# An attention and feed-forward kernel whose first product is done with seven block products in four of six chunks

## The chip, the cores and the metric

The kernel runs on one core of a Trainium2 chip. A core has TensorE (PE, matrix products; PEld is its loading of weights), VectorE (DVE), ScalarE (ACT), GpSimd (POOL) and SyncE (SP), which issues most transfers. SBUF is the working memory of 128 partitions, PSUM the memory of eight banks into which TensorE writes. The metric is the device time of one execution in microseconds; less is better.

## The reference

A local attention with block summaries is followed by a feed-forward layer without a choice of experts. Cut to what matters:

```python
# q, k, v: (4, 8, 768, 64); w_in: (512, 2048); w_out: (2048, 512)
k_sum = k.reshape(B, H, 24, 32, D).max(axis=3)
v_sum = v.reshape(B, H, 24, 32, D).mean(axis=3)
scores_l = q @ k.T / 8, kept where |i - j| < 16
scores_s = q @ k_sum.T / 8 + log(32)
a = softmax(concat(scores_l, scores_s))
x = (a @ concat(v, v_sum)) as (3072 tokens, 512)
h = x @ w_in
g = h * erf(softplus(h))
out = g @ w_out
```

All data are float32, and the output is too.

## The kernel before

**Tiles.** The 3072 tokens are cut into six chunks of T = 512, and the 2048 hidden columns into four groups of 512. A period k stands for one chunk and one group (ch = k // 4, g = k % 4), so there are 24 periods. A unit of weights is 128x2x512, half a megabyte in float32; each is held as two fp32r parts, high and low, 1 MB for both together.

**Products.** The first product `mm1(k, f)` makes h transposed: 128 hidden columns (f = 0 to 3) by 512 tokens, summed over four parts of x (cc = 0 to 3). Each part costs three matmuls, high by high, high by low and low by high, so a period has 4 x 4 x 3 = 48 matmuls of 128x512 at L635. The second product `mm2(k)` adds to four banks o0 to o3 with 48 more at L700; in the first two periods it is done in plain f32 with fewer matmuls (L696). The four results of mm1 go alternately into the banks h0 and h1; `hout` (L640) copies them to the tile hc, 128x1024 for two of them (n = 0, 1).

**Between the products.** softplus(h) is made of Tanh (L650), Ln (L659) and then Erf (L664) on ScalarE; Exp for the softmax (L541) runs on it too. They need different function tables, which L899 loads. `gsplit` multiplies by h on VectorE (L676), casts to the high part gh (L275) and subtracts for the low part gl (L683). hc, gh and gl have one buffer for each half n, so gh of a period can be written only when the second product of the period before has read it.

**Attention.** A quad is one chunk and one pair of heads, 24 in all. Each period from k = 4 to 19 turns, applies and splits quad k + 4 (`transp`, L571; `av`, L596; `xsplit`, L602 to L614) and scores quad k + 5 (`scores`, L500; `softmax`, L517 to L561). Scores and turned probabilities share a double bank, pa; av writes into h0 or h1. xsplit leaves x as xh and xl for each head pair.

**Order.** Each operation is registered in a `Plan` with its engines and planned cost, and with names that it reads and writes. `Plan.order` (L100) places them one at a time, by the engine that is free first, and by a due time (L79) plus a shift from the table TUNE (L44). TensorE's operations may leave their order of registration by up to 60 places among the first 330, and not at all afterwards. Every engine's queue is then executed in that order. In periods 4 to 23 TensorE's registered order is mm1 with attention between, and then mm2 of the period before (L843 to L870).

**Weights.** SBUF has 14 slots, w0 to w13. w_in stays in w0 to w7. Of w_out, parts m = 0 to 3 stay in slots from period 4 or 5 on; m = 4 to 7 go to DRAM once (`put`, L355) and come back into the slots 10 and 8 (`get`, L363) when the second product has read what was there.

**End.** After the last period mm2 runs alone, and `evac_last` (L718) copies and stores the output in halves.

Of the kernel before, what the change touches and what calls it, by code (L numbers as in the profile page):

```python
# [40 lines left out]
NN = 2  # L41
TABLE = 1.29
# [10 lines left out]
class Plan:  # L53
# [6 lines left out]
    def add(self, eng, fn, r=(), w=(), after=(), table=None, hold=0.0, beside=None):  # L60


        n, deps = len(self.ops), set(after)
        for x in r:
# [12 lines left out]
        return n  # L77
# [107 lines left out]
def block_attention_mlp(ctx: ExitStack, tc: tile.TileContext, q_t, k_nat, k_win, v_tok, v_nat, v_win, w_in, w_out, out):  # L185
# [87 lines left out]

    def copy(e, o, i):
        e.copy(o, i) if e is nc.scalar else e.tensor_copy(o, i)  # L275
# [79 lines left out]
    def put(m, n):  # L355
        u = ("o", m // 2, m % 2)

        def go():
# [4 lines left out]
    def get(m):  # L363
        u, n = ("o", m // 2, m % 2), HOME[m]

        def go():
            t = slot(n, [128, 2, 2, 512], F32R, "w")
            whl[u] = t[:, 0], t[:, 1]
            nc.sync.dma_start(out=f32(t), in_=dr[m])
        dma(1049, go, [f"d{m}"], frees(n), hold=0.0)  # L370


    rows = sb([128, 2 * S], F32, "rows")
# [228 lines left out]
    def xsplit(qd, eng):  # L602
        ch, p = divmod(qd, NP)
        n, s = qd % NX, st[qd]

        def high(e):
            xt[ch, p] = [sb([128, T], F32R, m, f"{m}{n}") for m in ("xh", "xl")]
            copy(e, xt[ch, p][0], s["xo"])

        def low(e):  # L610
            st.pop(qd)
            e.tensor_tensor(xt[ch, p][1], s["xo"], f32(xt[ch, p][0]), op=ALU.subtract)
        on(eng, high, [s["bank"]], [f"xh{n}"])
        on({"DVE": 0.6}, low, [s["bank"], f"xh{n}"], [f"xl{n}"])  # L614


    hs, wt, hc, gs, os_ = {}, {}, {}, {}, {}
# [22 lines left out]
    def hout(k, f, eng):  # L640
        bank, s = hbank(k, f), f // 2

        def hcopy(e):
            if f % 2 == 0:
                hc[k, s] = sb([128, 2, T], F32, "hc", f"hc{s}")
            copy(e, hc[k, s][:, f % 2], hs[k, f][:, 0:T])

        def tanh():
            wt[k, s] = sb([128, 2, T], F32, "wt", f"wt{s}")
            nc.scalar.activation(wt[k, s], hc[k, s], AF.Tanh, scale=0.5)  # L650
        on(eng, hcopy, [bank], [f"hc{s}"])
        if f % 2:
            act(0.96, tanh, [f"hc{s}"], [f"wt{s}"], table=("sig", "exp"))

    def logs(k):

        for n in range(2):
            s = f"wt{n}"
            act(1.06, lambda n=n: nc.scalar.activation(wt[k, n], wt[k, n], AF.Ln, scale=-0.49999994, bias=half_b), [s], [s], table=("log",))  # L659

    def erfs(k, after):
        for n in range(2):
            s = f"wt{n}"
            act(0.96, lambda n=n: nc.scalar.activation(wt[k, n], wt[k, n], AF.Erf, scale=-1.0), [s], [s], table=("sig",), after=after)  # L664
# [23 lines left out]
    def mm2(k, fs=range(G), ts=range(NT)):  # L688
        ch, g = divmod(k, NG)

        def go(i, t):
            if g == 0 and i == 0:
                os_[ch, t] = tiles[f"o{t}"] = ps("ops", f"o{t}")
            x, first, last = gs[k, i // 2], g == 0 and i == 0, g == NG - 1 and i == G - 1
            if k < NN:
                nc.tensor.matmul(os_[ch, t], lhsT=x[0][:, i % 2, t * 128:(t + 1) * 128], rhs=w32["o", g, i // 2][:, i % 2], start=first, stop=last)  # L696
                return
            w = [t[:, i % 2] for t in whl["o", g, i // 2]]
            for n, (m, y) in enumerate(((0, 0), (0, 1), (1, 0))):
                nc.tensor.matmul(os_[ch, t], lhsT=x[y][:, i % 2, t * 128:(t + 1) * 128], rhs=w[m], start=first and n == 0, stop=last and n == 2)  # L700
        for i in fs:
            for t in ts:
                m = 2 * g + i // 2
                if k < NN:
                    pe(0.868, lambda i=i, t=t: go(i, t), [f"a{m}", f"gh{i // 2}"], [f"o{t}"])
                else:
                    pe(0.681, lambda i=i, t=t: go(i, t), [f"w{HOME[m] if ch else FIRST[m]}", f"gh{i // 2}", f"gl{i // 2}"], [f"o{t}"])

# [102 lines left out]
    early = 5  # L811
    early_att = {(1, 1): [(lambda n: follow(n, "o2"), 4)], (1, 3): [(attend, 4), (follow, 5)],
                 (2, 1): [(output, 4), (attend, 5), (follow, 6)], (2, 3): [(output, 5), (attend, 6), (follow, 7)],
                 (3, 1): [(output, 6), (attend, 7), (follow, 8)], (3, 3): [(output, 7), (attend, 8), (follow, 9)]}

    for k in range(NPER):
        qa, qs = k + NP, k + NP + 1
        ch, g = divmod(k, NG)
        mult = sub = {"DVE": 1.136}
        cast = {"DVE": 0.605}  # L820
# [8 lines left out]
        if k == 4:  # L829
            parts(0, 9)  # L830
        if k == 5:
            for m in (1, 2, 3):
                parts(m, HOME[m])
        if k < NG:
            for f in range(G):
                if k and f % 2 == 0:
                    gsplit(k - 1, f // 2, mult, cast, sub)
                if k:
                    mm1(k, f)
                hout(k, f, heng)  # L840
                for what, n in early_att.get((k, f), []):
                    what(n)
        else:  # L843
# [17 lines left out]
            if qa < NQ:  # L861
                xsplit(qa, xeng)
# [6 lines left out]
        if k:  # L869
            mm2(k - 1)  # L870
# [70 lines left out]
```

## Time and profile before

| | us |
|---|---|
| median of 3 runs | 638.03 |
| lowest and highest | 636.91, 638.83 |
| profiled execution, first to last instruction (span) | 635.3 |
| TensorE busy in it | 629.0 |
| VectorE busy | 392.0 |
| ScalarE busy | 431.7 |
| POOL busy | 19.6 |

The span lies 2.7 us under the median of the runs: it counts from the first to the last instruction. Of the 24 periods the ones from k = 8 to 18 take about 25 us each, and the last ones, without attention, 21.8. In a row of groups stand line, engine, operation, tile, shape and count; then busy time and the mean of one instruction, and the idle time ahead of them. In the chain, start and length stand ahead of engine, tile and line. In a row of windows stand the limits and the length, the busy time of the five engines in order, the granted clock, the DMA engines' share and GB/s.

### The profile page before, as it was taken

What the parts mean: (1) busy time and instruction counts of PE and PEld (TensorE: products, weight loads), DVE (VectorE), ACT (ScalarE), POOL (GpSimd) and SP (SyncE); (2) the same over time, 40 slices, a digit from 0 to 9 for tenths busy, and PEclk for the clock granted to TensorE, in tenths of its full rate; (3) what the DMA queues carried; (4) which work ended last, traced back from release to release, by engine and by line L of the source; (5) the groups of instructions that cost most, each with busy time, mean ns of one, the idle gap of its engine ahead of it and who ended that gap; (6) DMA issues with size and microseconds to landing.
All of it is one profiled execution on the core that took longest, in us unless ns stands there. A gap on an engine that the chain in (4) does not pass through costs nothing.

```text
span 635.3 us, 10484 instructions
## 1 busy us (share of the span) xinstructions
PE 629.0 (99%) x4264; PEld 502.0 (79%) x4264; DVE 392.0 (62%) x502; ACT 431.7 (68%) x742; POOL 19.6 (3%) x56
## 2 busy tenths in 40 slices
PE   8999999999999999999999999999999999999997
PEld 6776557888888887888888888888888888888886
DVE  4999999756766647676655645735555454334442
ACT  5669977978949648976484684674954952863470
POOL 2001010100000000000000000000000000000000
PEclk9999999999999999999999999999999999999999
DMA  9998947724641334653152640224451103140013
GB/s 320 259 375 299 349 160 243 263 83 164 213 131 48 104 98 158 237 153 104 51 164 82 206 143 1 79 71 142 145 180 32 32 1 132 67 133 0 2 63 135
DMA packets 28483, 89.30 MB, mean 141 GB/s; under 512 B 3028, under 2 KB 8468, under 8 KB 23316
## 3 DMA queue, kind: packets, MB, share of 16 engines
q1 hardware_dynamic: 27860, 88.13, 41.9%
q8 instruction: 33, 0.54, 0.4%
q10 hardware_dynamic: 576, 0.52, 0.2%
q14 instruction: 14, 0.11, 0.1%
HBM read 75.89 MB, written 10.49 MB: 136 GB/s over the span
## 4 chain that ended last, share of the span: by engine, by line
PE 96%; DMA 2%; SPq 0%; ACT 0%; issue 0%; DVE 0%; ACTq 0%
PE h L635 41%; PE ops L700 38%; PE ops L696 4%; PE px L596 4%; PE pa L500 3%; PE pa L571 3%; DMA rw<-w_in 1%; PE vs L437 1%; DMA qf<-q_t 1%; PE idle L738 1%; PE vt L395 0%; SPq L445 0%; PE pa L491 0%; PE o L500 0%; PE h L500 0%
## 5 line engine op out<-in xcount | busy, mean ns | idle before, releaser
L635 PE MATMUL h<-xh,w 128*128 128x512 f32 x768 | 253.4, 396 | 0.0
L700 PE MATMUL ops<-w,gh 128*128 128x512 f32 x704 | 227.9, 393 | 0.0
L635 PEld LDWEIGHTS h<-xh,w 128*128 128x128 f32 x768 | 144.2, 188 | 32.1 <-issue 1.6
L700 PEld LDWEIGHTS ops<-w,gh 128*128 128x128 f32 x704 | 132.4, 188 | 28.4 <-issue 0.6
L635 PE MATMUL h<-xl,w 128*128 128x512 f32 x384 | 149.5, 389 | 0.0
L650 ACT ACTIVATE wt<-hc 128x1024 f32<-128x1024 f32 x48 | 50.7, 1057 | 136.5 <-DVE hc L275 136.4
L700 PE MATMUL ops<-w,gl 128*128 128x512 f32 x352 | 137.1, 390 | 0.0
L899 ACT ACT_TABLE_LOAD x105 | 134.7, 1283 | 1.9
L275 DVE COPY hc<-h 128x512 f32<-128x512 f32 x81 | 55.7, 690 | 124.0 <-PE h L635 123.4
L635 PEld LDWEIGHTS h<-xl,w 128*128 128x128 f32 x384 | 72.2, 188 | 15.1 <-issue 1.0
L700 PEld LDWEIGHTS ops<-w,gl 128*128 128x128 f32 x352 | 66.1, 188 | 13.0
L676 DVE TENSOR_TENSOR hc<-wt,hc 128x1024 f32<-128x1024 f32 x44 | 52.9, 1221 | 19.1 <-ACT wt L664 19.1
L659 ACT ACTIVATE wt<-wt,stats 128x1024 f32<-128x1024 f32 x48 | 55.4, 1153 | 0.6
L683 DVE TENSOR_TENSOR gl<-hc,gh 128x1024 fp32r<-128x1024 f32 x44 | 52.9, 1221 | 0.6
L541 ACT ACTIVATE pr<-pr,stats 128x120 f32<-128x120 f32 x128 | 48.7, 382 | 5.5 <-DVE stats L550 5.4
L664 ACT ACTIVATE wt<-wt 128x1024 f32<-128x1024 f32 x48 | 49.8, 1058 | 0.4
L275 DVE CAST gh<-hc 128x1024 fp32r<-128x1024 f32 x44 | 30.0, 692 | 28.0 <-PE ops L700 27.1
L575 ACT COPY ptr<-pa 120x1024 f32<-120x1024 f32 x24 | 24.2, 1009 | 12.0 <-PE px L596 6.5
L696 PE MATMUL ops<-a32s,gw 128*128 128x512 f32 x64 | 29.2, 595 | 0.0
L463 POOL COPY kw<-ksum 128x96 f32<-128x96 f32 (+1 forms) x28 | 14.8, 544 | 440.4 <-DMA kw<-k_win 440.4
L525 DVE TENSOR_TENSOR pr<-pa,mask_sb 128x960 f32<-128x960 f32 x16 | 18.5, 1157 | 10.3 <-PE pa L500 10.3
L596 PEld LDWEIGHTS px<-ptr,vw 120*64 120x64 f32 x640 | 20.3, 138 | 5.3 <-DVE hc L275 1.6
(110 smaller groups left out, 499.1 us busy)
## 6 DMA issues: line engine op xcount, KB each, us to landing
w<-dr SPq DMA_DIRECT2D x20, 1024.0 KB
kw<-k_win SPq DMA_DIRECT2D x20, 480.0 KB
rw<-w_in SPq DMA_DIRECT2D x8, 1024.0 KB
rw<-w_out SPq DMA_DIRECT2D x8, 1024.0 KB
vw<-v_win SPq DMA_DIRECT2D x20, 384.0 KB
qb<-q_t SPq DMA_DIRECT2D x20, 256.0 KB
rows<-k_nat SPq DMA_DIRECT2D x12, 384.0 KB
rows<-v_nat SPq DMA_DIRECT2D x12, 384.0 KB
```

The costliest lines, as they stand in the source:

```text
L275: e.copy(o, i) if e is nc.scalar else e.tensor_copy(o, i)
L541: nc.scalar.activation(s["pr"][:, j], s["pr"][:, j] if qd >= MQ else s["sc"][j // NI][:, i * NK:(i + 1) * NK], AF.Exp, scale=0.125, bias=s ...
L596: nc.tensor.matmul(xo[r, o], lhsT=s["vw"][:, j, r], rhs=s["pt"][:, a, o], start=True, stop=True)
L635: nc.tensor.matmul(hs[k, f][:, 0:T], lhsT=w[m], rhs=xt[ch, cc][x], start=(cc == 0 and n == 0), stop=(cc == 3 and n == 2))
L650: nc.scalar.activation(wt[k, s], hc[k, s], AF.Tanh, scale=0.5)
L659: act(1.06, lambda n=n: nc.scalar.activation(wt[k, n], wt[k, n], AF.Ln, scale=-0.49999994, bias=half_b), [s], [s], table=("log",))
L664: act(0.96, lambda n=n: nc.scalar.activation(wt[k, n], wt[k, n], AF.Erf, scale=-1.0), [s], [s], table=("sig",), after=after)
L676: e.tensor_tensor(hc[k, n], wt.pop((k, n)), hc[k, n], op=ALU.mult)
L683: e.tensor_tensor(gs[k, n][1], hc.pop((k, n)), f32(gs[k, n][0]), op=ALU.subtract)
L696: nc.tensor.matmul(os_[ch, t], lhsT=x[0][:, i % 2, t * 128:(t + 1) * 128], rhs=w32["o", g, i // 2][:, i % 2], start=first, stop=last)
L700: nc.tensor.matmul(os_[ch, t], lhsT=x[y][:, i % 2, t * 128:(t + 1) * 128], rhs=w[m], start=first and n == 0, stop=last and n == 2)
L899: nc.scalar.preload_act_table_set(sets[o["load"]])
```

## The change

In the last four chunks (k = 8 to 23, `FAST = 8`) the first product is cut into 2 x 2 blocks. The 512 tokens are split into a left and a right half of 256 (L and R), the four parts of x into two pairs (0, 1 and 2, 3), and the hidden columns of a group into two blocks j for each half n. Eight block products are replaced by seven (Strassen's scheme in Winograd's form). The seven need sums of weight blocks, S1 to S4, and of x blocks, T1 to T4. As registered, a period has 14 jobs (P1 to P7 for n = 0 and 1) of six matmuls of 128x256. P1 and P6, P7 and P4 follow one another in one half bank, P5 and P3 in another, each added to what stands there; between them the state is copied or added into hc. The half n = 0 uses the banks h0 and h1, the half n = 1 the two banks of pa (now named pA and pB in the plan).

The sums of weights are made in periods 5 to 7 (`add_up`), on VectorE or POOL, split into high and low parts, and stored in DRAM. From then on all of w_out and the sums are loaded each period (`get`, `get_sums`) into five slots in turn (w12, w13, w11, w9, w8), four loads of 1 MB a period. The T blocks are made from the result of `av` in `xsplit_fast`, kept unsplit in slot 10, and once a chunk `tsplit` writes their high and low parts over the weight blocks that the seven products don't use.

From period 4 on (`SOFT = 4`) softplus is one ScalarE function with its own table, Softplus in place of Tanh, and Ln is left out. In periods 5 to 7 copies of h may go to ScalarE as well as VectorE, in 4 to 7 the cast to gh too. From period 8 on, both gsplit are registered first, then the products, then the second product of the period before with attention between its parts. TUNE keeps its entries 0 to 463, and the later ones are dropped.

```diff
+SOFT = 4
+FAST = 8
...
-    HOME = {0: 9, 1: 12, 2: 11, 3: 13, 4: 10, 5: 8, 6: 10, 7: 8}
+    LATER = {0: 12, 1: 13, 2: 9, 3: 8, 4: 9, 5: 8}
+    ROUND = (12, 13, 11, 9, 8)
+    SUMS, TURN, RAW_X = 11, (12, 13), 10
...
+    def add_up(g):
...
+        sum_eng = {"DVE": 0.66, "POOL": 1.3}
+        for i, (r, j) in ((0, (0, 0)), (3, (1, 1)), (2, (0, 1)), (1, (1, 0))):
+            on(sum_eng, lambda e, i=i, r=r, j=j: whole(e, i, r, j), w[r:r + 1] + ([] if i == 0 else [f"w{SUMS}"]), (frees(SUMS) if i == 0 else []) + [f"s{i}"])
+        for o, x, y, op in ((3, 2, 3, ALU.add), (2, 0, 2, ALU.subtract), (0, 3, 0, ALU.subtract), (1, 1, 0, ALU.subtract)):
+            on(sum_eng, lambda e, o=o, x=x, y=y, op=op: plus(e, o, x, y, op), [f"s{x}", f"s{y}", f"w{SUMS}"], [f"s{o}"])
+        i = [f"s{n}" for n in range(4)] + [f"w{SUMS}"]
+        for n in range(2):
+            act(1.05, lambda n=n: high(n), i, frees(TURN[n]))
+            on({"DVE": 1.22}, lambda e, n=n: low(e, n), i + [f"w{TURN[n]}"], [f"w{TURN[n]}"])
+            dma(1049, lambda n=n: out_(n), [f"w{TURN[n]}"], [f"ds{g}{n}"], hold=3.0)
...
+    def get_sums(g, n):
+        m = sum_at[g, n] = turn()
...
+        dma(1049, go, [f"ds{g}{n}"], frees(m), hold=0.0)
...
+    def xsplit_fast(qd):
...
+        if p < 2:
+            on(either, high, [b], [f"xh{n}"])
+            on(either, right, [b], [f"r{T3}{c}"])
+            on({"DVE": 0.45}, one, [b, f"r{T3}{c}"], [f"r{T1}{c}"])
+            on({"DVE": 0.45}, low, [b, f"xh{n}"], [f"xl{n}"])
+        else:
+            on({"DVE": 0.45}, two, [b, f"r{T1}{c}"], [f"r{T2}{c}"])
+            on({"DVE": 0.45}, three, [b], [f"r{T3}{c}"])
+            on({"DVE": 0.69, "ACT": 0.59}, high, [b], [f"xh{n}"])
+            on({"DVE": 0.69}, low, [b, f"xh{n}"], [f"xl{n}"])
+            on({"DVE": 0.45}, four, [b, f"r{T2}{c}"], [f"r{T4}{c}"])
...
+    def tsplit(i):
...
+        act(0.59, high, [f"r{i}0", f"r{i}1"], [f"T{i}"])
+        on({"DVE": 0.66}, low, [f"r{i}0", f"r{i}1", f"T{i}"], [f"U{i}"])
...
+            for c in range(2):
+                w, y = what(n, c)
+                shape = o.rearrange("p (n f) -> p n f", n=2) if len(y[0].shape) == 3 else o
+                for i, (m, l) in enumerate(((0, 0), (0, 1), (1, 0))):
+                    nc.tensor.matmul(shape, lhsT=w[m], rhs=y[l], start=first and c == 0 and i == 0, stop=c == 1 and i == 2, skip_group_check=True)
...
+            "P1": ("b", lambda n, c: (win(0, 0, n, c), xs(c, L)), L, True, lambda n: [W0] + X0),
+            "P2": ("a", lambda n, c: (win(1, 0, n, c), xs(2 + c, L)), L, True, lambda n: [W1] + X1),
+            "P6": ("b", lambda n, c: (wsum(S2, n, c), ts(T2, c)), L, False, lambda n: [f"w{sum_at[g, n]}", f"T{T2}", f"U{T2}"]),
+            "P5": ("a", lambda n, c: (wsum(S1, n, c), ts(T1, c)), R, True, lambda n: [f"w{sum_at[g, n]}", f"T{T1}", f"U{T1}"]),
+            "P7": ("b", lambda n, c: (wsum(S3, n, c), ts(T3, c)), L, False, lambda n: [f"w{sum_at[g, n]}", f"T{T3}", f"U{T3}"]),
+            "P3": ("a", lambda n, c: (wsum(S4, n, c), xs(2 + c, R)), R, False, lambda n: [f"w{sum_at[g, n]}"] + X1),
+            "P4": ("b", lambda n, c: (win(1, 1, n, c), ts(T4, c)), L, False, lambda n: [W1, f"T{T4}", f"U{T4}"]),
...
+        def out3(n):
+            on({"DVE": 0.69}, lambda e: e.tensor_tensor(hc[k, n][:, 0], bank(n, "a"), hc[k, n][:, 0], op=ALU.add), [pair_banks(n)[0]], [f"ha{n}", f"hb{n}"])
...
+        for name in ("P1a", "P1b", "P2a", "P2b", "P6a", "P5a", "P6b", "P5b", "P7a", "P3a", "P7b", "P3b", "P4a", "P4b"):
+            name, n = name[:2], "ab".index(name[2])
+            job(name, n)
+            if name in outs:
+                outs[name](n)
...
-        for n in range(2):
+        for n in range(2 if k < SOFT else 0):
...
+            for n in range(2):
+                gsplit(k - 1, n, mult, cast, sub)
+            products(k)
+            mm2(k - 1, (0,))
...
+        if NG < k < FAST:
+            for x in {5: (1,), 6: (2, 3), 7: (0,)}[k]:
+                add_up(x)
+        if k >= FAST - 1:
+            if k + 1 < NPER:
+                for n in range(2 if k >= FAST else 0):
+                    get_sums((k + 1) % NG, n)
             for r in range(2):
-                get(6 + r if g == 3 else 4 + r)
+                get(2 * (k % NG) + r, turn())
```

More of the change, by code (lines that the diff above doesn't have):

```diff
@@ L63, in add @@
         n, deps = len(self.ops), set(after)
+        r, w = ([y for x in z for y in (("pA", "pB") if x == "pa" else (x,))] for z in (r, w))
         for x in r:
@@ L356, in put @@
         u = ("o", m // 2, m % 2)
+        w_at[u] = n
         def go():
@@ L370, in get, with block, whole, plus @@
         dma(1049, go, [f"d{m}"], frees(n), hold=0.0)
+    w_at = {("o", m // 2, m % 2): n for m, n in FIRST.items()}
+    w_sum, sum_at, turns = {}, {}, [0]
+    S2, S4, S3, S1 = range(4)
+    def block(g, r, j):
+        return [kept["i", g, r][:, m].rearrange("p c (n j f) -> p n j c f", n=2, j=2)[:, :, j] for m in range(2)]
+    def add_up(g):
+        w, s = [f"w{2 * g}", f"w{2 * g + 1}"], {}
+        def whole(e, i, r, j):
+            if i == 0:
+                s["t"] = slot(SUMS, [128, 2, 4, 2, 128], F32, "sums")
+            h, l = block(g, r, j)
+            e.tensor_tensor(s["t"][:, :, i], f32(h), f32(l), op=ALU.add)
+        def plus(e, o, x, y, op):
+            e.tensor_tensor(s["t"][:, :, o], s["t"][:, :, x], s["t"][:, :, y], op=op)
+        def high(n):
+            t = s["hl", n] = slot(TURN[n], [128, 2, 4, 2, 128], F32R, "ws")
+            if g == 0:
+                w_sum[g, n] = t
+            nc.scalar.copy(t[:, 0], s["t"][:, n])
+        def low(e, n):
+            e.tensor_tensor(s["hl", n][:, 1], s["t"][:, n], f32(s["hl", n][:, 0]), op=ALU.subtract)
+        def out_(n):
+            dr["s", g, n] = dram.tile([128, 2, 4, 2, 128], F32, name=f"ds{g}{n}", tag=f"ds{g}{n}")
+            nc.sync.dma_start(out=dr["s", g, n], in_=f32(s["hl", n]))
+        sum_eng = {"DVE": 0.66, "POOL": 1.3}
[8 more added lines that the diff above has]
+            dma(1049, lambda n=n: out_(n), [f"w{TURN[n]}"], [f"ds{g}{n}"], hold=3.0)
+            if g == 0:
+                sum_at[g, n] = turn()
@@ L373, in block_attention_mlp, with turn, go @@
+    def turn():
+        turns[0] += 1
+        return ROUND[(turns[0] - 1) % len(ROUND)]
+    def get_sums(g, n):
+        m = sum_at[g, n] = turn()
+        def go():
+            t = w_sum[g, n] = slot(m, [128, 2, 4, 2, 128], F32R, "ws")
+            nc.sync.dma_start(out=f32(t), in_=dr["s", g, n])
+        dma(1049, go, [f"ds{g}{n}"], frees(m), hold=0.0)
     rows = sb([128, 2 * S], F32, "rows")
@@ L614, in xsplit, with rough, high, right @@
         on({"DVE": 0.6}, low, [s["bank"], f"xh{n}"], [f"xl{n}"])
+    L, R = slice(0, T // 2), slice(T // 2, T)
+    T1, T2, T3, T4 = range(4)
+    raw = []
+    def rough(i, c):
+        if not raw:
+            raw.append(slot(RAW_X, [128, 4, 2, T // 2], F32, "traw"))
+        return raw[0][:, i, c] if c is not None else raw[0][:, i]
+    def xsplit_fast(qd):
+        ch, p = divmod(qd, NP)
+        n, s, c, b = qd % NX, st[qd], p % 2, st[qd]["bank"]
+        either = {"DVE": 0.45, "ACT": 0.4}
+        def high(e):
+            xt[ch, p] = [sb([128, T], F32R, m, f"{m}{n}") for m in ("xh", "xl")]
+            copy(e, xt[ch, p][0][:, L] if p < 2 else xt[ch, p][0], s["xo"][:, L] if p < 2 else s["xo"])
+        def right(e):
+            copy(e, rough(T3, c), s["xo"][:, R])
+        def low(e):
+            z = L if p < 2 else slice(0, T)
+            e.tensor_tensor(xt[ch, p][1][:, z], s["xo"][:, z], f32(xt[ch, p][0])[:, z], op=ALU.subtract)
+        def one(e):
+            e.tensor_tensor(rough(T1, c), rough(T3, c), s["xo"][:, L], op=ALU.subtract)
+        def two(e):
+            e.tensor_tensor(rough(T2, c), s["xo"][:, R], rough(T1, c), op=ALU.subtract)
+        def three(e):
+            e.tensor_tensor(rough(T3, c), s["xo"][:, R], rough(T3, c), op=ALU.subtract)
+        def four(e):
+            st.pop(qd)
+            e.tensor_tensor(rough(T4, c), s["xo"][:, L], rough(T2, c), op=ALU.subtract)
+        if p < 2:
[9 more added lines that the diff above has]
+            on({"DVE": 0.45}, four, [b, f"r{T2}{c}"], [f"r{T4}{c}"])
@@ new lines, in place, with view, high, low @@
+    def place(i, m):
+        return kept["i", i, 0][:, m].rearrange("p c (n j f) -> p j c n f", n=2, j=2)[:, 1]
+    def tsplit(i):
+        def view():
+            return rough(i, None).rearrange("p c (n f) -> p c n f", n=2)
+        def high():
+            nc.scalar.copy(place(i, 0), view())
+        def low(e):
+            e.tensor_tensor(place(i, 1), view(), f32(place(i, 0)), op=ALU.subtract)
+        act(0.59, high, [f"r{i}0", f"r{i}1"], [f"T{i}"])
+        on({"DVE": 0.66}, low, [f"r{i}0", f"r{i}1", f"T{i}"], [f"U{i}"])
@@ L649, in tanh, with soft @@
             wt[k, s] = sb([128, 2, T], F32, "wt", f"wt{s}")
-            nc.scalar.activation(wt[k, s], hc[k, s], AF.Tanh, scale=0.5)
+            if k < SOFT:
+                nc.scalar.activation(wt[k, s], hc[k, s], AF.Tanh, scale=0.5)
+            else:
+                nc.scalar.activation(wt[k, s], hc[k, s], AF.Softplus)
         on(eng, hcopy, [bank], [f"hc{s}"])
         if f % 2:
-            act(0.96, tanh, [f"hc{s}"], [f"wt{s}"], table=("sig", "exp"))
+            soft(k, s, tanh)
+    def soft(k, s, fn):
+        act(0.96 if k < SOFT else 1.06, fn, [f"hc{s}"], [f"wt{s}"], table=("sig", "exp") if k < SOFT else ("soft",))
@@ L663, in erfs @@
             s = f"wt{n}"
-            act(0.96, lambda n=n: nc.scalar.activation(wt[k, n], wt[k, n], AF.Erf, scale=-1.0), [s], [s], table=("sig",), after=after)
+            act(0.96, lambda n=n: nc.scalar.activation(wt[k, n], wt[k, n], AF.Erf, scale=-1.0 if k < SOFT else 1.0), [s], [s], table=("sig",), after=after)
     def gsplit(k, n, mult, cast, sub):
@@ L700, in go @@
                 nc.tensor.matmul(os_[ch, t], lhsT=x[y][:, i % 2, t * 128:(t + 1) * 128], rhs=w[m], start=first and n == 0, stop=last and n == 2)
+        at = [w_at.get(("o", g, r)) for r in range(2)]
         for i in fs:
@@ L819, in block_attention_mlp @@
         mult = sub = {"DVE": 1.136}
-        cast = {"DVE": 0.605}
+        cast = {"DVE": 0.605, "ACT": 0.95} if NG <= k < FAST else {"DVE": 0.605}
         xeng, heng = ({"DVE": 0.6, "ACT": 0.48},) * 2 if k < early else ({"DVE": 0.6},) * 2
@@ L829, in block_attention_mlp @@
         if k == 4:
[L830 to L833, printed above, removed]
+            for m in (2, 3):
+                parts(m, LATER[m])
+            for c in range(2):
+                for i in range(4):
+                    P.last[f"r{i}{c}"], P.readers[f"r{i}{c}"] = [], [y for x in frees(RAW_X) for y in P.readers.get(x, [])]
         if k < NG:
@@ L842, in block_attention_mlp @@
                     what(n)
-        else:
+        elif k < FAST:
             gsplit(k - 1, 0, mult, cast, sub)
@@ L890, in block_attention_mlp @@
     plan = P.order(free, lambda n: 60 if n < 330 else 0, TUNE, "exp")
-    sets = {"exp": "exp_and_others", "log": "natural_log_exp_and_others", "sig": "sigmoid_and_others"}
+    sets = {"exp": "exp_and_others", "log": "natural_log_exp_and_others", "sig": "sigmoid_and_others", "soft": "softplus"}
     filling = True
```

107 lines of the change are left out of this document (98 added, 9 removed).

## The prediction

> **What bounds the kernel now.** I read the page first: the engines' shares and the chain that ended last.
>
> ```profile
> span 635.3 us, 10484 instructions
> PE 629.0 (99%) x4264; PEld 502.0 (79%) x4264; DVE 392.0 (62%) x502; ACT 431.7 (68%) x742; POOL 19.6 (3%) x56
> PE 96%; DMA 2%; SPq 0%; ACT 0%; issue 0%; DVE 0%; ACTq 0%
> ```
>
> TensorE (PE) is never without work after the start, and the chain runs through it. A busy PE need not be a PE at its peak, so I looked at the chain in order of time, which gives the steps from one instruction to the next, and at the instructions on tile h, which belong to the first product.
>
> ```profile
> L635 PE MATMUL h<-xh,w x512: 388/389/496, 238.6 to 609.6; 128*128 128x512 f32 x171
> L635 PE MATMUL h<-xl,w x256: 387/389/395, 238.8 to 609.3; 128*128 128x512 f32 x128
> ...
> 52.43 6.87 PE ops L696 x16
> ...
> 484.83 5.44 PE h L635 x24
> 490.27 0.87 PE pa L571 x8
> 491.14 5.48 PE h L635 x24
> 496.63 0.98 PE pa L500 x32
> 497.61 1.08 PE px L596 x32
> 498.69 11.11 PE ops L700 x48
> 509.80 5.44 PE h L635 x24
> ...
> 599.07 10.88 PE h L635 x48
> 609.95 21.77 PE ops L700 x96
> ```
>
> The last 16 periods (k = 8 to 23, the four chunks that change) hold 512 + 256 = 768 matmuls of the first product, from 238.6 us on. In k = 18 one piece starts where the last ended: 24.97 us, with 10.9 for the first product, 2.9 for attention and 11.1 for the second. A matmul is recorded with 389 ns, but 48 of them advance the chain by 10.88: 0.2267 us each. That step counts. Every tenth of a microsecond that TensorE saves in a period is a tenth off the time, as long as nothing else becomes late.
>
> What the other engines have to spare, by windows (k = 4 to 7; k = 8 to 18; k = 19 on) and by groups:
>
> ```profile
> 138.00:236.00 98.00, 98.00 (x665) 79.81 (x664) 63.52 (x83) 72.94 (x129) 1.77 (x4) 1.00 0.38 127
> 236.00:509.80 273.80, 273.80 (x1845) 225.53 (x1845) 159.28 (x209) 187.26 (x322) 4.98 (x14) 1.00 0.36 115
> 509.80:621.00 111.20, 111.20 (x523) 91.98 (x522) 47.03 (x54) 61.10 (x55) 0.00 (x0) 1.00 0.17 57
> ...
> 434.90:459.90 25.00, 25.00 (x169) 20.61 (x169) 13.63 (x19) 17.39 (x31) 0.35 (x1) 1.00 0.42 135
> ```
>
> The columns after the length are PE, PEld, DVE, ACT and POOL busy, the granted clock (1.00, so no throttle) and the DMA share. VectorE (DVE) works 58% in the middle stretch, ScalarE (ACT) 68%, DMA 36%.
>
> **The change, part by part.**
>
> *Matmuls.* A period's first product was 48 matmuls of 512 tokens; now it is 14 jobs (P1 to P7 for two halves) of 6, so 84 of 256 tokens: seven eighths of the columns. No fp32r matmul of 256 columns stands in the trace. The nearest rows, from the timeline and the groups:
>
> ```profile
> 25.59 1.70 PE L738 MATMUL idle<-zeros 128*128 128x256 bf16 x14
> 27.14 1.09 PE L571 MATMUL pa<-ident,prf 128*120 128x128 f32 x8
> ...
> L635 PEld LDWEIGHTS h<-xh,w 128*128 128x128 f32 x768 | 144.2, 188 | 32.1 <-issue 1.6 <-ACT hc L275 0.6
> L571 PEld LDWEIGHTS pa<-ident,pr 128*120 128x120 f32 x160 | 18.4, 136 | 3.2 <-issue 0.6 <-PE vt L395 0.2
> ```
>
> Low end: the transposes of L571 advance by 0.87/8 = 0.109, and 14 bf16 matmuls of 256 columns by (27.14 - 25.59)/14 = 0.111; half of 0.2267 is 0.113. Towards the high end: if the f32 matmuls of L696 (6.87/16 = 0.429 a step) stream at half rate, 512 columns alone cost 0.215, so an fp32r matmul has 0.012 of its own; 256 columns are then 0.107 + 0.012 = 0.119. The outer end is the weight load: with 188 ns as its occupancy it would set the step. I take 0.120, since L635 is the row of the same kind. 84 x 0.120 = 10.08 against 10.88 to 10.92: **0.81 us a period, 13.0 us over 16**. At 0.113 it would be 1.36 and 21.8; nothing is left at 10.89/84 = 0.130.
>
> *The weight load.* TensorE then loads weights 84 times a period in place of 48, each under a matmul half as long. The L571 rows show a record of 136 ns with a step of 109, so the records overlap and aren't occupancy; scaled from 120 to 128 columns the step is at most 0.109 x 128/120 = 0.116. [...] Sharing weights is no help either way: each matmul has its own load, 4264 of each.
>
> *Evacuations and their waits.* Four PSUM copies of 128x512 a period (DVE) become eight copies of 128x256 (out1, out6, out5, out4; DVE or ACT), two adds of 128x256 (out7) and two of 128x512 (out3). Prices:
>
> ```profile
> L275 DVE COPY hc<-h 128x512 f32<-128x512 f32 x81 | 55.7, 690 | 124.0 <-PE h L635 123.4 <-DVE gl L683 0.5
> L275 DVE COPY rows<-ops 128x256 f32<-128x256 f32 x3 | 1.3, 426 | 7.1 <-ACT rows L275 7.1
> L275 ACT COPY rows<-ops 128x256 f32<-128x256 f32 x3 | 1.1, 373 | 12.7 <-PE ops L700 12.7
> L612 DVE TENSOR_TENSOR xl<-px,xh 128x512 fp32r<-128x512 f32 x24 | 16.4, 685 | 0.5 <-ACT xh L275 0.3
> L683 DVE TENSOR_TENSOR gl<-hc,gh 128x1024 fp32r<-128x1024 f32 x44 | 52.9, 1221 | 0.6
> DVE gh L275 <- PE ops L700: 27.1, 10, 3.2
> ```
>
> An add of 128x256 stands in no row; 0.43 as the copy, between 0.34 (half of 685) and 0.69. DVE: the 13.63 us of the period at 434.9 lose 2.76 and gain 2.24, half of the copies (1.7), 0.9 for the longer split of x (2.7 in place of 1.37 for two of four head pairs, 1.8 for the others) and 0.7 for the T blocks: 16.4, or 18.1 with all copies, of 24.2 us. It isn't the bound by its sum.
>
> But TensorE now waits for DVE and ACT inside the product: P6 adds onto P1's bank after out1 has read it, P7 after out6, P3 after out5, P4 after out7. Each has three jobs between, 3 x 0.72 = 2.16 us; take 0.43 and hand-overs of 0.2, and 1.5 is left for what stands ahead in DVE's queue. One long operation (1.22) fits, two don't. Behind the waiting matmul stands all of TensorE. Seven operations of 1.15 to 1.22 a period make DVE long-busy some 35% of the time; a pair ahead of one of the eight hand-overs then comes 8 x 0.35 x 0.35 = 1 time, at some 0.2 over: **0.2 us a period, 3.2 us**. Bounds: 0, and 1.22 for one missed operation a period. Besides, out1 of the second half needs gl done with hc, and gh (0.69) waits for the second product's last matmul, as the last row shows it already; 0.69 + 1.22 + 0.43 = 2.34 before P6b at 6 x 0.72 = 4.32. That fits.
>
> *ScalarE.* Tanh, Ln and Erf become Softplus and Erf from k = 4 on.
>
> ```profile
> L650 ACT ACTIVATE wt<-hc 128x1024 f32<-128x1024 f32 x48 | 50.7, 1057 | 136.5 <-DVE hc L275 136.4
> L659 ACT ACTIVATE wt<-wt,stats 128x1024 f32<-128x1024 f32 x48 | 55.4, 1153 | 0.6
> L664 ACT ACTIVATE wt<-wt 128x1024 f32<-128x1024 f32 x48 | 49.8, 1058 | 0.4
> L899 ACT ACT_TABLE_LOAD x105 | 134.7, 1283 | 1.9
> ```
>
> Softplus is bounded by 1.06 and 1.15. Two Ln (2.3) go, and three tables a period (softplus, sigmoid, exp; 3.85) stand against 4 to 5. Worth nothing on the path: ScalarE is hidden under TensorE. After a product the chain is Softplus 2.1, a load 1.28, Erf 2.1, DVE 3.1: 8.6 us, under 10.9 of the second product even at the end of the kernel, where the next product no longer covers it. So the tail stays: gh waits there for mm2 as now.
>
> *DMA.* Four blocks of 1.05 MB a period are loaded (two of w_out, two of sums) in place of one to two. One such load alone on the engines:
>
> ```profile
> 434.00:436.00 2.00, 2.00 (x10) 1.65 (x10) 1.87 (x4) 0.00 (x0) 0.00 (x0) 1.00 0.32 59
> 436.00:438.00 2.00, 2.00 (x11) 1.65 (x10) 2.00 (x3) 0.00 (x0) 0.00 (x0) 1.00 0.74 303
> 438.00:440.00 2.00, 2.00 (x11) 1.65 (x10) 0.48 (x1) 0.00 (x0) 0.00 (x0) 1.00 0.46 188
> ...
> SPq L369 <- PE ops L700: 175.1, 19, 56.7
> ```
>
> 2 x (0.32 + 0.74 + 0.46) = 3.04 us of all engines. The period at 434.9 has 0.42 x 25.0 = 10.5, two such loads among it, so 4.4 for attention. New: 4 x 3.04 + 4.4 = 16.6, and up to 19.5 with k and v rows and output: 69 to 81% of 24.2 us. A slot is free a period less half a product ahead of its use, 17 us or more against 3 to 12 in the queue. Cost 0. SyncE's queue waits in order for slots (the last row); behind a waiting load stand kw, vw and q, whose buffers come free 20 us before they are read. If that cover goes, TensorE waits for a load: 3 us each.
>
> *Preparation, k = 5 to 7.* Four add_up: 32 two-operand operations of 128x512 (DVE 0.69, or POOL), 8 lows (1.22), 8 copies on ACT, 8 stores. DVE had 63.5 of 98 us; lows add 9.8, the split of x 3.5, all sums 22: 98.8, more than there is. POOL must take some, and shows one-operand copies only:
>
> ```profile
> L443 POOL COPY vwf<-vsum 24x1024 f32<-24x1024 f32 x1 | 1.1, 1107 | 15.8 <-ACT vsum L440 15.8
> ```
>
> Half of it, 0.55, to 2.2 for two operands; I take 1.1. With half of the sums on POOL, DVE stands at 88 of 98. The four rounds share one slot and end in the block that P6 of k = 8 needs. Cost between 0 and 11 (a round late, at most one second product); I take **1.8**, since a round is some 9 us (3.5 for eight sums on two engines, 3.5 for copies and lows, 2 of hand-overs), which fits four times in three periods of 25, and the order of TensorE can still move there. [...]
>
> **Sum:** -13.0 + 3.2 + 1.8 = -8.0. Span 635.3 - 8.0 = 627.3; the median of the runs, 638.03, lies 2.7 above the span, so **630.0 us**.
>
> **Rivals.**
> 1. *Half-length matmuls cost half* (0.113 a step): 21.8 saved, 5 lost: 621. For it: L571 and L738. Against it: 0.2267 itself has something beyond streaming, which may be per instruction. Chance 0.20.
> 2. *Hand-overs in PSUM* (slower): DVE's in-order queue misses them twice a period. Two operations of 1.2 cost 2.4, less 0.81, times 16, and 1.8: 638.0 + 25.4 + 1.8 = 665; it decides from 0.8 us of waiting a period, where it gives 640. For it: 35% of DVE in long operations, no double buffer in four banks. Against it: 1.5 us of room each, ACT as second engine. Chance 0.17.
> 3. *The new blocks come late* (add_up on DVE and POOL, or loads in the queue): some 8 us more than taken, 638, no change. Chance 0.14, of which I put 0.06 faster, 0.06 same, 0.02 slower.
> 4. *The load isn't hidden:* 84 x 0.188 = 15.8, 4.9 more a period, 79 in all: 717. The L571 step speaks against it. Chance 0.03.
>
> **Numbers.** The forecast of 622 to 636 has 0.46. A measurement of this kernel tells 0.3% (1.9 us) from no change. Faster: 0.46 + 0.20 + 0.06 = 0.72; same 0.06; slower 0.02 + 0.17 + 0.03 = 0.22. The range, 614 to 646, takes in rivals 1 and 3 and the mild half of 2.
>
> **What would show it.** Right: 1344 matmuls of 128x256 from about 237 us on in place of 768 of 128x512, a job of six advancing the chain by 0.72, periods of 24.2 to 24.4 us, TensorE at 98% or more, ACT with three table loads a period. A job of 0.68 speaks for rival 1, of 1.1 for rival 4. Idle TensorE released by DVE or ACT hc speaks for rival 2; released by DMA, or a gap at 237 to 245 us, for rival 3. Wrong altogether would be a DVE over 90% busy from k = 8 on, or DMA shares near 1.

## The result: 1.2% slower

The changed kernel takes 646.32 us (median of 4 runs, 641.93 to 647.84), the kernel before 638.32 beside it: a ratio of 1.0123, with a 95% interval from 1.0087 to 1.0159. It is slower: 0.3 us outside the range of the prediction (614 to 646) and on the other side of its forecast.

The page of the changed kernel, with the rows that answer to those of before:

```profile
span 645.0 us, 12021 instructions
PE 622.7 (97%) x4840; PEld 522.6 (81%) x4840; DVE 432.1 (67%) x607; ACT 406.7 (63%) x804; POOL 39.7 (6%) x68
...
PE 78%; DVE 11%; DMA 5%; ACT 3%; issue 1%; SPq 0%; DVEq 0%; ACTq 0%
```

The span grew by 9.7 us, a little more than the medians (8.0). TensorE sat idle for 22.3 us in place of 6.3, and the chain, 96% TensorE before, now runs 22% of the span outside it: VectorE, transfers and ScalarE. The mean granted clock is 0.995; it was 1.00 in every stretch read before.

Where in the kernel was the time lost? The start of a period's first product is a good ruler. Three starts in the chain of the kernel before, those of k = 9, 12 and 20:

```profile
259.80 5.44 PE h L635 x24
...
334.88 5.44 PE h L635 x24
...
533.79 10.88 PE h L635 x48
```

and the same three in the timeline of TensorE of the changed kernel, where P1 is the job that reads w and xh into hb:

```profile
266.95 0.28 PE L808 MATMUL hb<-xh,w 128*128 128x256 f32 x1
...
344.94 0.28 PE L808 MATMUL hb<-xh,w 128*128 128x256 f32 x1
...
543.67 0.28 PE L808 MATMUL hb<-xh,w 128*128 128x256 f32 x1
```

The last two columns hold the two variants of the changed kernel that say most (e2 and e6 below), with their starts read in the same way.

| stretch, us | before | after | e2 | e6 |
|---|---|---|---|---|
| up to k = 9 | 259.80 | 266.95 | 266.12 | 257.35 |
| k = 9 to 11 | 75.08 | 77.99 | 74.47 | 72.74 |
| k = 12 to 19 | 198.91 | 198.73 | 192.67 | 192.67 |
| k = 20 to the end | 101.5 | 101.3 | 98.4 | 98.4 |
| span | 635.3 | 645.0 | 631.7 | 621.2 |

So there are two questions. In the quiet periods from k = 12 on, the change should have saved 0.8 us each and saved 0.02. And 10.1 us were lost before k = 12.

**The quiet periods.** One first product in the chain of the changed kernel, in order of time:

```profile
470.06 0.71 PE hb L808 x6
...
477.25 1.46 PE pa L808 x12
...
478.80 0.42 DVE hc L858
479.22 0.61 DVE hc L861
...
479.87 0.98 PE pa L808 x6
480.86 2.75 PE ops L922 x12
```

A job of six advances the chain by 0.71 to 0.72, as forecast. But the fourteen take 480.86 - 470.06 = 10.80 us and not 14 x 0.72 = 10.08. Ahead of the last job (P4 of the half n = 1, into pa) the chain leaves TensorE for two adds on VectorE: out7 (L858) and out3 (L861). The waits of TensorE, summed over the run (total, times, longest), name the same:

```profile
PE pa L808 <- DVE hc L861: 7.2, 14, 1.0
```

There are 14 waits for out3, which reads the *other* bank of pa; P4 needs only out7. The timeline of the same place one period on, TensorE and then VectorE, shows why (in brackets the idle time ahead and who ended it):

```profile
502.01 0.88 PE L808 MATMUL pa<-w,ws 128*128 128x256 f32 x6
502.73 0.28 PE L808 MATMUL pa<-xh,ws 128*128 128x256 f32 x1
...
503.45 0.88 PE L808 MATMUL hb<-w 128*128 128x256 f32 x6
504.79 0.98 PE L808 MATMUL pa<-w 128*128 128x256 f32 x6 [0.47 <-DVE hc L861]
505.61 0.40 PE L922 MATMUL ops<-w,gh 128*128 128x512 f32 x1
...
503.72 0.42 DVE L858 TENSOR_TENSOR hc<-pa,hc 128x256 f32<-128x256 f32 x1 [0.82 <-PE pa L808]
504.06 0.68 DVE L861 TENSOR_TENSOR hc<-pa,hc 128x512 f32<-128x512 f32 x1
```

P7 of n = 1 runs from 502.01 to 502.73 by its step, P3 from 502.73 to 503.45. out7 needs P7 alone; yet VectorE, idle for 0.82 us, starts it at 503.72, when P3 has ended too. In the half n = 0, whose banks h0 and h1 are two tiles, no such wait appears. The half n = 1 uses the two banks of **one tile**, pa: a reader of one bank waits for the matmuls into the other, and a matmul into one for the readers of the other. From 503.45 to 505.61 the last two jobs take 2.16 us in place of 1.44: **0.72 us a period are lost**, nearly the whole 0.81 that the matmuls saved.

**Up to k = 9.** Windows of 2 us around the two places where TensorE falls dry (columns as before: PE, PEld, DVE, ACT, POOL, granted clock, DMA share, GB/s):

```profile
164.00:166.00 2.00, 0.62 (x6) 0.38 (x4) 1.79 (x2) 2.00 (x4) 0.00 (x0) 1.00 0.56 220
166.00:168.00 2.00, 1.48 (x33) 1.04 (x33) 1.90 (x3) 2.00 (x5) 0.00 (x0) 1.00 0.02 5
168.00:170.00 2.00, 1.44 (x3) 1.00 (x4) 2.00 (x3) 1.98 (x4) 0.00 (x0) 0.54 0.79 180
170.00:172.00 2.00, 2.00 (x7) 1.60 (x6) 1.97 (x3) 1.99 (x2) 1.14 (x1) 0.60 1.03 341
...
242.00:244.00 2.00, 0.59 (x5) 0.38 (x4) 2.00 (x4) 0.04 (x1) 0.00 (x0) 1.00 1.03 414
244.00:246.00 2.00, 0.68 (x5) 0.69 (x6) 2.00 (x3) 0.65 (x2) 0.00 (x0) 1.00 1.07 344
246.00:248.00 2.00, 2.00 (x13) 1.85 (x12) 1.83 (x3) 0.95 (x3) 0.00 (x0) 0.67 0.93 291
248.00:250.00 2.00, 2.00 (x12) 2.00 (x11) 0.00 (x1) 0.37 (x1) 0.00 (x0) 0.50 0.84 356
```

TensorE is idle for some 2.5 us at 164 to 169 and for 2.7 at 242 to 246, and each time the granted clock then falls, to 0.50 in the last of these windows, for 3 to 4 us: (1 - 0.54) x 2 + (1 - 0.60) x 2 = 1.7 us at the first place, and 0.66 + 1.00 = 1.7 at the second. The chain into the second gap:

```profile
233.61 3.14 ACT pr L605 x16
...
239.01 1.07 ACT wt L886
...
240.10 1.28 DVE hc L898 x2
...
243.67 1.14 DVE gl L905
...
244.89 0.38 ACT hc L278
...
245.32 0.98 PE hb L808 x6
```

Erf (L886) of k = 7 stands behind the Exp of the softmax (L605), with a cast of sums and a table load between them; then VectorE makes gh and gl, and only then is hc free for out1 of k = 8, for which P6 waits. Exp goes first because the program says so for k = 4 to 7 (the argument of `erfs`); the kernel before has the same rule, but there pieces of the second product (L700, from 248.07 us in its timeline) stand between those of the first product of k = 8, and TensorE waits for nothing from 225 to 260 us. Now the first product of k = 8 stands, up to its last job, ahead of that second product. The chain into the first place has the same links: Exp until 161.3 us, a copy and a table load, Erf from 163.1, VectorE until 168.5. For the first part of that gap, 1.5 us ahead of the scores at 166.13, the profile names nobody ("issue").

**k = 9 to 11.** The chain into the gap of 1.5 us at 295:

```profile
277.01 8.71 DMA out<-rows
...
285.74 7.84 DMA rows<-v_nat
...
293.67 0.95 DVE vs_sum L452
...
294.70 0.86 DVE ksum L451
295.56 0.60 DVE gh L278
...
296.55 0.98 PE hb L808 x6
```

A quarter-megabyte store of the output and the load of rows after it take 16.6 us together; the load goes into columns of the tile `rows` that the store reads, and is issued (at 285.74 us) when the store has landed. The window over the two, in the changed kernel, has the DMA engines at 0.96 (0.34 in the same window of the kernel before):

```profile
276.00:294.00 18.00, 17.53 (x149) 14.80 (x148) 9.52 (x13) 10.17 (x12) 0.00 (x0) 1.00 0.96 333
```

VectorE stands before the reduction of these rows (vs_sum, idle for 3.54 us ahead of it in the timeline), and ksum, gh and out1 are queued behind it.

### The profile page after: what moved, and what is told of

Same layout as the page of the kernel before. It is cut to its first block, busy times and chain, and to the rows that moved or that the text cites. A ratio compares the mean times of both kernels' runs of the same rounds, so it can differ in the third digit from the quotient of the medians.

```text
span 645.0 us, 12021 instructions
## 1 busy us (share of the span) xinstructions
PE 622.7 (97%) x4840; PEld 522.6 (81%) x4840; DVE 432.1 (67%) x607; ACT 406.7 (63%) x804; POOL 39.7 (6%) x68
## 4 chain that ended last, share of the span: by engine, by line
PE 78%; DVE 11%; DMA 5%; ACT 3%; issue 1%; SPq 0%; DVEq 0%; ACTq 0%
PE ops L922 31%; PE pa L808 12%; PE h L763 11%; PE hb L808 5%; PE ha L808 5%; PE ops L918 4%; PE px L660 3%; PE pa L635 3%; PE pa L564 2%; DMA out<-rows 2%; DVE hc L861 1%; DVE hc L898 1%; DMA rows<-k_nat 1%; DMA rows<-v_nat 1%; DVE hc L858 1%
## 5 line engine op out<-in xcount | busy, mean ns | idle before, releaser
L763 PE MATMUL h<-xh,w 128*128 128x512 f32 x256 | 86.9, 405 | 0.3 <-ACT hc L278 0.3
L278 ACT COPY hc<-hb 128x256 f32<-128x256 f32 x35 | 13.1, 373 | 85.9 <-PE hb L808 50.1
L763 PEld LDWEIGHTS h<-xh,w 128*128 128x128 f32 x256 | 48.6, 190 | 12.7 <-ACT hc L278 1.5
L605 ACT ACTIVATE pr<-pr,stats 128x120 f32<-128x120 f32 x128 | 48.8, 382 | 8.6 <-DVE stats L614 8.4
L763 PE MATMUL h<-xl,w 128*128 128x512 f32 x128 | 50.2, 393 | 0.0
L886 ACT ACTIVATE wt<-wt 128x1024 f32<-128x1024 f32 x48 | 50.0, 1058 | 0.3
L278 DVE CAST gh<-hc 128x1024 fp32r<-128x1024 f32 x40 | 27.8, 697 | 23.5 <-PE ops L922 23.2
L808 PE MATMUL pa<-w,ws 128*128 128x256 f32 x288 | 41.0, 287 | 0.8 <-DVE hc L278 0.8
L808 PEld LDWEIGHTS pa<-w,ws 128*128 128x128 f32 x288 | 37.4, 194 | 1.3 <-DVE hc L278 1.2
L808 PE MATMUL hb<-w,ws 128*128 128x256 f32 x192 | 29.1, 288 | 4.3 <-ACT hc L278 2.7
L278 ACT CAST xh<-px 128x512 fp32r<-128x512 f32 (+1 forms) x20 | 10.2, 512 | 36.0 <-PE px L660 36.0
L874 ACT ACTIVATE wt<-hc 128x1024 f32<-128x1024 f32 x32 | 32.1, 1052 | 0.2
L808 PEld LDWEIGHTS hb<-w,ws 128*128 128x128 f32 x192 | 25.9, 196 | 4.7 <-ACT hc L278 2.9
```

What stands on the lines that cost most here:

```text
L605: nc.scalar.activation(s["pr"][:, j], s["pr"][:, j] if qd >= MQ else s["sc"][j // NI][:, i * NK:(i + 1) * NK], AF.Exp, scale=0.125, bias=s ...
L763: nc.tensor.matmul(hs[k, f][:, 0:T], lhsT=w[m], rhs=xt[ch, cc][x], start=(cc == 0 and n == 0), stop=(cc == 3 and n == 2))
L808: nc.tensor.matmul(shape, lhsT=w[m], rhs=y[l], start=first and c == 0 and i == 0, stop=c == 1 and i == 2, skip_group_check=True)
L874: nc.scalar.activation(wt[k, n], hc[k, n], AF.Softplus)
```

## Experiments

Three theories for the loss: **the tile** (both banks of pa count as one), **the preparation** (Erf behind Exp, with the slow clock after the gap), and **the late rows**. The rivals: VectorE simply misses the hand-overs, with its queue full of long operations (the second rival of the prediction); the dropped entries of TUNE spoil the order of the first periods; ScalarE's new function matters after all. Where an expectation gives theories letters, C is the late rows and D the dropped entries of TUNE. All of the first four ran on one chip (before: 637.77), the other four on another (before: 637.72). The changed kernel itself was timed only beside the 638.32 above, so a difference from it compares medians of two occasions, on which the kernel before lay 0.6 us apart.

**e1: another order of the jobs.** The last P3 of n = 0 goes between P3 and P4 of n = 1, so that out7 and out3 of n = 1 have one more job of time.

```diff
-        for name in (... "P7a", "P3a", "P7b", "P3b", "P4a", "P4b"):
+        for name in (... "P7a", "P7b", "P3b", "P3a", "P4a", "P4b"):
```

> The changed kernel with the last six jobs of a product in the order P7a, P7b, P3b, P3a, P4a, P4b. Theory A (both banks of pa are one tile: a reader of one bank waits for the matmuls into the other, and P4b for the add that reads the other): out7 and out3 of the second half now have two jobs ahead of P4b, so its wait of 0.47 us in the profile (0.7 us in the chain) goes; 16 x 0.7 = 11 us less, about 635. Rival B (VectorE is simply late in the product): the wait moves to another job and the time stays within 2 us of the changed kernel, 644 to 648.

It took 640.22 us (ratio to before 1.0032, 1.0013 to 1.0052): 6.1 less than the changed kernel, between the two expectations. The quiet period falls from 24.92 to 24.66 only. The chain of this kernel shows where the rest stayed:

```profile
471.50 1.45 PE pa L808 x12
...
472.97 0.44 DVE hc L278
...
473.43 0.38 ACT hc L278
...
473.86 1.70 PE pa L808 x12
```

At 471.50 stand P6 and P5 of n = 1, both into pa. Their copies out6 and out5 start when both have ended, and P7, which now comes one job earlier, waits for both. The wait moved to the pair before: the order shares out the loss, it doesn't remove it.

**e2: pa as two tiles.** The order stays; the two banks become tiles pa and pb. The softmax's add of the mask and ScalarE's copy of the turned probabilities, which took both banks at once, are done in two instructions each.

```diff
-return psum.tile([128, 2, 512] if tag == "pa" else [128, 512], F32, name=name, tag=tag)
+return psum.tile([128, 512], F32, name=name, tag=tag)
...
-t = tiles["pa"] = ps("pa", "pa")
-where_[1, "a"], where_[1, "b"] = t[:, 0], t[:, 1]
+where_[n, x] = ps("hp"[n] + x, pair_banks(n)["ab".index(x)])
```

> The changed kernel with its own order of jobs, but pa as two tiles of one bank each (the softmax add and the copy of turned probabilities then take two instructions each). Theory A: out7 of the second half starts when P7b ends, one job earlier, P4b doesn't wait, and the time falls by 16 x 0.7 = 11 us to about 635, as with the other order; two more instructions in VectorE and ScalarE take 0.1 to 0.2 us a period off the path. Rival B: no change within 2 us. If the order helps and the two tiles don't, A is wrong about the tile.

It took 634.05 us (0.9936, 0.9912 to 0.9960): 12.3 less than the changed kernel, and 0.6% faster than before. The same place in its timeline, TensorE and then VectorE:

```profile
444.66 0.88 PE L807 MATMUL pb<-w,ws 128*128 128x256 f32 x6
...
446.10 0.88 PE L807 MATMUL hb<-w 128*128 128x256 f32 x6
446.82 0.88 PE L807 MATMUL pb<-w 128*128 128x256 f32 x6
447.54 0.40 PE L921 MATMUL ops<-w,gh 128*128 128x512 f32 x1
...
445.58 0.42 DVE L857 TENSOR_TENSOR hc<-pb,hc 128x256 f32<-128x256 f32 x1
```

out7 now starts 0.2 us after P7's six steps, beside P3, and the last two jobs take 447.54 - 446.10 = 1.44. The eight periods from k = 12 take 192.67 in place of 198.73, 0.76 less each. VectorE does more work than in the changed kernel (the split instructions), and in these periods TensorE doesn't wait for it: the rival of the full queue falls.

**e3: the late rows.** e1, and the plan counts the rows of the last batch as landing 6 us later, so that VectorE's order puts other work ahead of their reductions.

```diff
-dma(393, lambda: nc.sync.dma_start(out=knat, in_=k_nat[b, p]), w=["ta", "tb"])
+dma(393, lambda: nc.sync.dma_start(out=knat, in_=k_nat[b, p]), w=["ta", "tb"], hold=8.0 if b == 3 else 2.0)
```

(and the same for v_nat)

> As e1_order, and the planned time of the k and v row loads of the last head pairs is 8 us in place of 2 behind their issue, so that VectorE gets the reductions that wait for them later in its queue. Theory C (in periods 9 to 11 VectorE stands before rows that are late in a full DMA queue, and the product behind it): 2 to 3 us below e1_order. Rival: the rows are not what holds it, no difference beyond 1 us.

It took 637.57 us (0.9996, 0.9979 to 1.0014), 2.65 less than e1. The gap before k = 10's P6, 1.04 us in e1, is gone, and k = 9 to 11 take 74.26 us against 75.70 in e1. So the profile shows 1.4 us for the rows; part of the 2.65 may be the spread of the runs, which is 5 us wide in both.

**e4: the kernel before with the shortened TUNE.** Nothing else is changed.

```diff
-TUNE = {0: (-833.887, 1.5, 0, None), ... 463: (95.3636, 1.5, 0, None), 464: (167.011, 1.5, 0, None), ...}
+TUNE = {0: (-833.887, 1.5, 0, None), ... 463: (95.3636, 1.5, 0, None)}
```

> The kernel before, with TUNE cut to its entries 0 to 463 and nothing else. Theory D (the loss near 165 us comes from the order that the dropped entries had set): TensorE idles some 2 us near 165 us and its clock drops for about 3 us afterwards, so 3 to 5 us slower, 641 to 643. Rival: the order without the entries is as good (all loss up to 250 us is the new work's), within 1 us of the kernel before.

638.16 us (1.0014, 0.9996 to 1.0032): no difference that can be told. It does open a gap, which the timeline of TensorE shows,

```profile
166.10 1.05 PE L500 MATMUL pa<-kw,qb 64*64 64x120 f32 x32 [1.64 <-issue]
```

at the same place as the first gap of the changed kernel, but the clock stayed at 1.00 behind it and the time was made up. The dropped entries are not where the 10 us went.

**e5: Erf no longer behind Exp.** The changed kernel, with the rule taken off in k = 4 to 7.

```diff
-erfs(k, [st[qs]["exps"]] if NG <= k < FAST and qs < NQ else [])
+erfs(k, [st[qs]["exps"]] if False and qs < NQ else [])
```

> The changed kernel without the rule that Erf of periods 4 to 7 comes after the Exp of the same period. Theory E (in the profile Erf of period 7 stands behind Exp, a copy of sums and a table load, so gsplit, hc and the product of period 8 are late; the same near 165 us): the gaps of 2.7 us at 245 and of 1.5 + 1.0 us near 166 go, and with them the stretches of half clock that follow (1.7 us each): 8 us less, about 638. Rival F (VectorE itself is full there with the sums, next to POOL): the gaps stay or move, within 2 us of the changed kernel.

636.68 us (0.9975, 0.9963 to 0.9987): 9.6 less than the changed kernel. In the timeline of TensorE, k = 9 starts 7.65 us earlier:

```profile
259.30 0.28 PE L808 MATMUL hb<-xh,w 128*128 128x256 f32 x1
```

Both gaps of the preparation are gone and the mean clock is 1.000 (0.995 in the changed kernel). The price of the two gaps was 2.5 + 2.7 us of idleness and 2 x 1.7 of half clock, 8.6; a new one of 1.27 us at 222 takes some back, and 7.3 is close to the 7.65. That new gap stands behind a copy of VectorE (hc, L278), so the rival of the expectation, a full VectorE, keeps a small part. k = 9 to 11 became shorter too, by 2.8 us, so what is lost there depends on what came before.

**e6: all three together.** e2, the hold of e3 and the rule of e5.

> Two tiles for pa, the later rows of e3 and the free Erf of e5 together. If A, C and E are separate losses they add: 634 from the two tiles, less 2.7, less 8, about 623 to 625, so 2% faster than the kernel before; that is the saving of 13 us of 84 x 0.120 against 10.9 a period. If they hide one another, 629 or more.

**623.59 us (0.9777, 0.9758 to 0.9797): 2.2% faster than the kernel before.** The engines' shares on its page:

```profile
PE 614.1 (99%) x4840; PEld 519.3 (84%) x4840; DVE 438.6 (71%) x630; ACT 412.0 (66%) x828; POOL 39.7 (6%) x68
```

and the window that the prediction read in the kernel before:

```profile
434.90:459.90 25.00, 25.00 (x213) 22.47 (x212) 16.02 (x27) 17.05 (x40) 0.35 (x1) 1.00 0.77 253
```

TensorE is busy without a break in that window, with the DMA engines at 0.77; the three periods from k = 9 on take 24.25 us each, and the eight from k = 12 on 192.67 as in e2. The three effects alone were 12.3, 2.65 and 9.6, in sum 24.6; together they give 22.7, which fits e5 having part of the late rows in it.

**e7: Softplus alone.** The kernel before with TUNE as in e4 and Softplus from k = 4 on; Ln is left out there.

```diff
-            nc.scalar.activation(wt[k, s], hc[k, s], AF.Tanh, scale=0.5)
+            if k < SOFT:
+                nc.scalar.activation(wt[k, s], hc[k, s], AF.Tanh, scale=0.5)
+            else:
+                nc.scalar.activation(wt[k, s], hc[k, s], AF.Softplus)
...
-        for n in range(2):
+        for n in range(2 if k < SOFT else 0):
```

> The kernel before with TUNE cut as in e4, and Softplus in place of Tanh and Ln from period 4 on, nothing else. ScalarE works some 2.3 us and one table load a period less. Theory (ScalarE is hidden under TensorE): within 1 us of e4, 637 to 639. Rival (ScalarE was late somewhere): 2 us or more faster than e4.

637.78 us (1.0000, 0.9985 to 1.0015), 0.4 below e4. The groups of this kernel have Softplus at

```profile
L654 ACT ACTIVATE wt<-hc 128x1024 f32<-128x1024 f32 x40 | 42.4, 1060 | 188.2 <-DVE hc L276 188.2
```

ScalarE's busy time falls from 423.9 us in e4 to 362.3, and nothing follows: 62 us off an engine that TensorE waited for only 0.3 us in the profile of the kernel before.

**e8: sums on VectorE alone.** e6, with POOL taken out of `add_up`. If what POOL costs VectorE were more than what it takes off, this would be as fast as e6 or faster.

```diff
-sum_eng = {"DVE": 0.66, "POOL": 1.3}
+sum_eng = {"DVE": 0.66}
```

> As e6, with all 32 sums of add_up on VectorE and none on POOL. The two products of wt and hc beside POOL's sums take 2.3 us each in the changed kernel; without POOL they should take 1.22. [...] Rival (VectorE has not enough time for 22 us of sums in three periods): gaps of 1 to 2 us of TensorE near 235 to 245, 3 to 5 us slower than e6.

One run: 626.77 us, 3.2 above the median of e6. In the groups of e8 a first sum of weights (L394) takes VectorE 0.69 us; in e6, beside POOL, the mean is 0.97; and none of the products of wt and hc takes over 1.37 us. POOL helps all the same, as far as one run can say: TensorE waits 0.76 us at 238 for VectorE and 1.26 at 246 for a block of w_out, whose load starts only behind the last low part of the sums, and the period k = 8 takes 27.15 us where e6 has 24.25. This is the place and the size that the rival of the expectation gave.

## Why the prediction failed

- **The saving was right.** 0.72 us a job, and with the waits gone (e2, e6) a quiet period goes from 24.97 to 24.2 us, 0.8 less, as worked out. The half-cost rival (0.68 a job) and the unhidden weight load (1.1) are out. A load is recorded with 189 to 196 ns (means of the groups) under a step of 120, so these records overlap still more than those of L571 (136 under 109).
- **The step that failed: "Each has three jobs between".** That counts jobs from the end of the job whose bank is read. It holds for n = 0, where each bank is a tile. For n = 1 it is miscounted already, as two jobs stand between P7 and P4 (P3 of n = 1 and P4 of n = 0); two are enough, as e2 shows, where no such wait is left. What counts for n = 1 is the time from the end of the *last* matmul into the tile to the end of the last reader of either bank: between P3 and P4 of n = 1 stands one job, 0.72 us, and into it had to go 0.42 of out7, 0.61 of out3 and the hand-overs. Charged were 0.2 us a period, measured 0.72 to 0.76; over 16 periods 11.5 to 12.2 against 3.2, and e2 gained 12.3. This is the place and nearly the price of the second rival (0.8, where it gave 640), by another mechanism: VectorE's queue was empty (idle for 0.82 us ahead of out7).
- **Mis-sized: the preparation**, 1.8 taken, 7.65 measured up to k = 9 and 9.6 in the time (e5). The bounds, 0 to 11, held it, but the reason was another: not a round of sums late, but Erf late behind Exp, where the second product no longer covered it. The question "who covers this now?" was asked at the tail and not at k = 8. And a gap was priced once; each of the two cost its length and, as estimated from the windows, 1.7 us of half clock. The 1.1 us for a sum on POOL, which is in the 1.8, was the author's estimate between 0.55 and 2.2, and no run shows it: in the changed kernel such a sum took 1.28 to 2.16 us.
- **Mis-sized: transfers**, 0 taken, 1.4 (k = 9 to 11) to 2.65 measured (e3). The streamed blocks themselves arrived in time; TensorE doesn't wait for one from k = 8 on. What the small store and the rows met was a DMA share of 0.96, near the 1 that the prediction named as a sign of being wrong, and their lateness reached TensorE through VectorE's queue. That it is the streamed blocks that fill the engines there is argued from the shares before and after (0.34, 0.96); no run took the blocks away.
- **Right: ScalarE is hidden** in the kernel before (e7) and in the quiet periods, though not at k = 8, where the chain runs through its Exp and Erf; the end is unchanged (25.35 to 25.30 us from the second product on), and VectorE isn't the bound: 16.8 us of the 25 at 434.9, where 16.4 were worked out.

The sum as it stands: -13.0 for the matmuls, some +12 for the tile, +9.6 for the preparation, +2.65 for the rows: +11, beside +8.0 in the medians and +9.7 between the profiles; the parts overlap by some 2, as e6 shows, and the rest is within the spread of the runs.

## What to carry to other kernels

Before one counts how many jobs lie between a write and its reader, one must look at what the program treats as one object: the two PSUM banks of the one tile pa had one set of waits, 0.72 us a period, and with a tile for each bank (e2) the accumulation in place, with readers in between, took 12.3 us less. (This is shown for the PSUM tile pa alone. In the SBUF tile `rows`, a load into other columns was issued at 279.31 us, while the store was still under way.) Moving a product ahead of the work that covered it shows its cost at the first place where the old order meets the new. A gap on TensorE is to be priced with the clock that the windows show behind it: here some 1.7 us after each of the four gaps of 2.7 to 2.8.

## What the hardware showed beside this

**Half clock after a gap.** In the profiles at hand each drop cost some 1.7 us, an estimate from windows of 2 us as above; the lowest window of each shows 0.50 to 0.54, and 1.7 us lost at 0.50 are 3.4 us of time. In the changed kernel a job of six then advances by 1.45 us (247.03 to 248.48) in place of 0.72. The drop came after all four gaps of 2.7 to 2.8 us near 245, in the changed kernel, e1, e2 and e3. After the pair of gaps at 164 to 171 (1.5 and 0.95 us in the changed kernel, 1.1 and 0.96 in e2) it came in these two, but not in e1 and e3, which have such a pair too. A single gap of 1.71 us at 35 brought it in e1, one of 1.64 in e4 and one of 1.54 at 295 in the changed kernel didn't. So the length of a gap alone doesn't tell these cases apart: the pair of 1.51 and 0.95 us brought the drop in the changed kernel and not in e1 and e3. What does tell them apart was not shown.

**VectorE beside POOL.** In the timeline of the changed kernel, VectorE and then POOL:

```profile
211.99 4.55 DVE L898 TENSOR_TENSOR hc<-wt,hc 128x1024 f32<-128x1024 f32 x2
...
211.09 4.37 POOL L397 TENSOR_TENSOR sums<-sums 128x512 f32<-128x512 f32 x2 [2.11 <-DVE sums L397]
```

Two multiplications that take 1.22 us each elsewhere take 2.3 beside POOL's adds, and those take 2.2 in place of 1.29, their shortest: both sides pay.
